# Attention beside an MLP on one core: one visit per head pair on 64x64 tiles, in place of separate phases

## The chip, the core and the metric

The kernel runs on one core of a Trainium2 chip. The metric is the device time of one execution in microseconds, the median of several runs. A profile is one further execution, and its span is a little shorter than the timed value. Engines are named as in the profile: PE (TensorE, the matrix engine), PEld (its weight loads), DVE (VectorE), ACT (ScalarE), POOL (GpSimd) and SP (SyncE, which here only issues transfers).

## What is computed

64 heads (8 batches of 8), each with 576 positions of 64 numbers. Every head has two attentions whose results are added: one over the means of four neighbouring positions (144 by 144), and one in which a position sees only neighbours less than four away. The result is the input of an MLP with a SiLU gate.

```python
q_d = q.reshape(B, H, Sd, factor, D).mean(axis=3)          # factor 4, likewise k_d, v_d
out_up = np.repeat(sm_attn(q_d, k_d, v_d), factor, axis=2)
mask = np.abs(pos[:, None] - pos[None, :]) < factor
scores = np.where(mask, scale * np.matmul(q, k.transpose(0, 1, 3, 2)), -1e9)
... softmax of scores ...
x = (out_up + np.matmul(attn, v)).transpose(0, 2, 1, 3).reshape(B * S, H * D)   # 4608 x 512
h = x @ w_in                                                # 512 x 2048
out = (h * (1.0 / (1.0 + np.exp(-h)))) @ w_out              # 2048 x 512
```

## The kernel before

Heads are worked on in pairs (32 pairs, 4 per batch). The program is written as one list of instructions per engine, with waits derived from what each reads and writes; a small scheduler in the source decides the order with rough costs. A pair goes through separate phases on PE, each with its own shape of tile. The phases of the pairs share two PSUM tiles, `duo0` and `duo1`, of two banks each; the MLP has `hps` (first layer, two banks) and `ops` (second layer, two banks).

```python
def load_v(p):                         # local attention: five overlapping windows of 128 keys
    win = bass.AP(..., ap=[[64, 128], [112 * 64, 5], [1, 64]])      # per head, into vs[128, 10, 64]
    ...                                # and vq[72, 4, 256]: four positions a row, for the means

def ph_T(p):                           # 6 + 6 transposes of 96 positions x 128 (both heads), then
    tps[:, 96 * c:96 * c + 96] <- transpose(w, id_bf)               # copies: q on DVE, k on ACT
def ph_S1(p):                          # scores, keys in rows: tiles 64x128, 2 heads side by side
    for c in range(4):
        for h in range(2):
            mm(D[:, h, QB[c]:QB[c] + NQ[c]], kT[rows, W0[c]:W0[c] + 128], qT[rows, ...])  # 120 or 112
def ph_S2(p): ...                      # fifth block, and 4 matmuls of 64x72 tiles for the means
# ACT: exp into Pt[128, 2, 576] and Pd[72, 2, 2, 144]; DVE: Pt *= mask
def ph_Z(z):                           # row sums of TWO pairs: 16 matmuls, tiles 128x32, weights all one
    mm(D[o:o + 32, 0, 0:360], ones_bf[:, 0:32], Pt[m][:, h, 0:360])
    mm(D[o:o + 32, 1, 0:216], ones_bf[:, 0:32], Pt[m][:, h, 360:576])
    for s in range(2):
        mm(D[o:o + 32, 1, 216:360], fours_bf[:, 0:32], Pd[m][:, h, s, :])
# ACT copies them to zc, 4 transfers bring them to zr[40, 72], DVE takes the reciprocal rr,
# 1 transfer writes it to DRAM (scr), 4 transfers read it back into Rb, spread over 64 partitions
def ph_PV(p):                          # 14 matmuls, tiles 128x64 (72x64 for the means)
    mm(D[64*h:64*h+64, ...], vb[:, 5 * h + c, :], Pt[:, h, QB[c]:QB[c] + NQ[c]])
    # DVE: xo = D * Rb in two instructions; POOL: xT = xo (local) + xo (means, four times each)
```

The first four pairs get their reciprocals another way: row sums into `hps`, a reciprocal on DVE, and a matmul that spreads them over partitions into `ops`.

```python
def g1(j, f):                          # first layer: 144 groups of four matmuls of 512 columns
    for kc in range(4): mm(hps[hb], w_in_sb[:, kc, 128*f:...], xT[:, kc, t0:t0 + 512])
    # ACT: th = tanh(h / 2); DVE: gT = (th + 1) * h
def g2(j, i):                          # second layer: 144 groups of four matmuls of 512 columns
    for f in range(4 * part, 4 * part + 4): mm(ops[ob], gT[:, f, 128*tt:...], w_out_bf[:, f, :])
    # after four groups ACT: osb = ops * 0.5, then a transfer to the output
```

The main loop of the scheduler takes an attention phase when one is ready (the same tile shape first), and an MLP group otherwise. Buffers: q and k 2 deep, v 2 deep, Pt and Pd 5, Rb 4.

The softmax here doesn't subtract the row's maximum and nothing guards it: scores larger than these inputs give would overflow.

## Time and profile before

| what | value |
|---|---|
| time, median of 3 runs | 417.98 us (415.85 to 418.28) |
| span of the profiled execution | 414.6 us, 6872 instructions |
| busy, share of span | PE 86%, PEld 52%, DVE 58%, ACT 52%, POOL 40% |
| largest groups on PE | hps 576 matmuls of 128x512, ops 576 (538 in the records) |
| chain that ended last, by engine | PE 58%, DMA 24%, SP's queue 5%, ACT 4%, DVE 3% |
| transfers | 65.62 MB in 80635 packets, of which 46812 under 512 B |
| sizes per transfer | vs 160 KB (x64), qs, ks and vq 288 KB (x32 each), Rb 180 KB (x56), output 256 KB (x36) |

How to read it: the busy share of PE is an average over a stage in which data is loaded, a stage in which attention and MLP share the engine, and a last stage of MLP alone. A matmul's record contains the time that it spends in the pipeline, so records overlap and PE looks busier than it is; counts of matmuls in a stretch of time say more. A share of a chain is the time of the steps that led, one releasing the next, to the last instruction.

### The profile page before, as it was taken

How to read it: one execution, taken by the hardware profiler on the slowest of the kernel's cores; microseconds unless marked ns; L12 is line 12 of the kernel's file. 1: busy time of each engine (PE TensorE's matmuls, PEld its weight loads, DVE VectorE, ACT ScalarE, POOL GpSimd, SP SyncE). 2: the span in 40 equal slices, each digit the busy share in tenths (PEclk: the TensorE clock that was granted, in tenths of full speed). 3: DMA queues.
4: the chain of work that ended last, by engine and by line, in shares of the span. 5: the costliest groups of instructions: out<-in, count | busy, mean ns of one | idle time of the engine just before them, and what ended most of it. 6: DMA issues, size and time to landing. Idle time of an engine off the chain costs nothing.

```text
span 414.6 us, 6872 instructions
## 1 busy us (share of the span) xinstructions
PE 356.2 (86%) x2682; PEld 215.0 (52%) x2720; DVE 240.9 (58%) x358; ACT 217.1 (52%) x375; POOL 165.4 (40%) x194
## 2 busy tenths in 40 slices
PE   3745467597939999999799999999999999999996
PEld 2422245364517656555455656565565555555552
DVE  4956334467646789687588776786546333333320
ACT  5551345356645767667578559648543344344331
POOL 7177185364436664567548277328004000000000
PEclk9968568988957999999999999999999999999999
DMA  7999999998568768989898994753151100101012
GB/s 209 258 217 321 224 216 213 209 202 217 160 185 201 183 161 187 251 178 225 208 235 204 231 248 106 211 159 78 53 145 52 52 25 25 52 25 51 27 51 76
DMA packets 80635, 65.62 MB, mean 158 GB/s; under 512 B 46812, under 2 KB 70364, under 8 KB 80604
## 3 DMA queue, kind: packets, MB, share of 16 engines
q1 hardware_dynamic: 75480, 57.38, 56.7%
q0 software_dynamic: 4224, 6.29, 6.7%
q10 hardware_dynamic: 900, 1.52, 1.4%
q8 instruction: 21, 0.34, 0.4%
q14 instruction: 10, 0.08, 0.1%
HBM read 57.51 MB, written 9.60 MB: 162 GB/s over the span
## 4 chain that ended last, share of the span: by engine, by line
PE 58%; DMA 24%; SPq 5%; ACT 4%; DVE 3%; issue 2%; POOL 2%; ACTq 1%; POOLq 0%
PE ops L340 26%; PE hps L340 24%; DMA vs<-in_v_dram 7%; DMA vq<-in_v_dram 6%; PE duo L340 5%; DMA scr<-rr 4%; DMA Rb<-scr 3%; PE duo L350 2%; DMA zr<-zc 2%; SPq L293 2%; ACT th L545 2%; DVE gT L547 2%; SPq L442 1%; DMA ks<-in_k_dram 1%; POOL vt L321 1%
## 5 line engine op out<-in xcount | busy, mean ns | idle before, releaser
L340 PE MATMUL hps<-xT,w_in_sb 128*128 128x512 f32 x576 | 180.2, 440 | 9.3 <-DVE gT L547 9.3
L547 DVE SCALAR_TENSOR_TENSOR gT<-th,hps 128x512 bf16<-128x512 f32 x144 | 98.3, 686 | 114.9 <-ACT th L545 114.5
L340 PE MATMUL ops<-w_out_bf,gT 128*128 128x512 bf16 x538 | 140.3, 383 | 6.2 <-DVE gT L547 2.6
L545 ACT ACTIVATE th<-hps 128x512 f32<-128x512 f32 x144 | 85.5, 597 | 105.4 <-PE hps L340 100.8
L340 PEld LDWEIGHTS hps<-xT,w_in_sb 128*128 128x128 f32 x576 | 109.0, 195 | 42.7 <-DVE gT L547 12.5
L340 PEld LDWEIGHTS ops<-w_out_bf,gT 128*128 128x128 bf16 x576 | 46.5, 98 | 66.9 <-issue 22.1
L522 POOL TENSOR_TENSOR xT<-xo 128x576 fp32r<-128x576 f32 (+2 forms) x40 | 40.2, 1018 | 79.5 <-DVE xo L505 79.2
L321 POOL TENSOR_TENSOR vt<-vq 72x512 f32<-72x512 f32 x32 | 43.0, 1342 | 32.3 <-DMA vq<-in_v_dram 31.2
L316 ACT ACTIVATE vb<-vs 128x640 bf16<-128x640 f32 x32 | 23.3, 735 | 29.6 <-DMA vs<-in_v_dram 26.4
L340 PE MATMUL duo<-qT,kT 64*128 64x112 bf16 (+1 forms) x320 | 21.5, 230 | 20.0 <-ACT Pd L391 7.3
L311 POOL CAST qb<-qs 96x768 bf16<-96x768 f32 x28 | 24.2, 865 | 33.0 <-PE duo L350 17.1
L397 DVE TENSOR_TENSOR Pt<-Pt,mask_bf 128x1152 bf16<-128x1152 bf16 x32 | 32.2, 1011 | 8.3 <-ACT Pt L389 8.3
L374 ACT ACTIVATE Pt<-duo 128x912 bf16<-128x912 f32 x32 | 29.5, 927 | 9.8 <-issue 4.9
L340 PEld LDWEIGHTS duo<-qT,kT 64*128 64x128 bf16 x320 | 11.5, 100 | 40.3 <-DVE xo L503 9.3
L566 ACT ACTIVATE osb<-ops 128x512 f32<-128x512 f32 x36 | 21.6, 599 | 19.5 <-PE ops L340 19.3
L355 DVE COPY qT<-duo 128x576 bf16<-128x576 bf16 x32 | 23.8, 748 | 13.4 <-PE duo L350 13.4
L350 PE MATMUL duo<-id_bf,qb 96*128 96x96 bf16 x192 | 15.5, 225 | 16.6 <-ACT Pt L374 8.0
L503 DVE TENSOR_TENSOR xo<-duo,Rb 128x456 f32<-128x456 f32 x32 | 20.0, 626 | 10.8 <-DMA Rb<-scr 6.2
L323 POOL TENSOR_TENSOR vd<-vt 72x256 bf16<-72x256 f32 x32 | 24.8, 776 | 2.5
L356 ACT ACTIVATE kT<-duo 128x576 bf16<-128x576 bf16 x32 | 20.8, 649 | 8.2 <-PE duo L350 8.2
L311 POOL CAST kb<-ks 96x768 bf16<-96x768 f32 x28 | 23.7, 845 | 2.7 <-DMA ks<-in_k_dram 2.7
L361 DVE TENSOR_REDUCE kd<-kT 128x144 bf16<-128x576 bf16 x32 | 23.8, 743 | 0.3 <-ACT kT L356 0.3
(48 smaller groups left out, 256.5 us busy)
## 6 DMA issues: line engine op xcount, KB each, us to landing
vs<-in_v_dram SPq DMA_DIRECT2D x64, 160.0 KB, 4.7
qs<-in_q_dram SPq DMA_DIRECT2D x32, 288.0 KB, 5.6
ks<-in_k_dram SPq DMA_DIRECT2D x32, 288.0 KB, 6.1
vq<-in_v_dram SPq DMA_DIRECT2D x32, 288.0 KB
out_dram<-osb SPq DMA_DIRECT2D x36, 256.0 KB, 2.2
Rb<-scr SPq DMA_DIRECT2D x48, 180.0 KB, 4.1
w_in_sb<-in_moe_w_in_dram POOLq DMA_DIRECT2D x4, 1024.0 KB, 13.1
w_out_bf<-in_moe_w_out_dram POOLq DMA_DIRECT2D x4, 512.0 KB, 10.7
```

Source lines behind the costliest of these rows:

```text
L311: pool(lambda g, d=dst, s=src: g.tensor_copy(d, s), r=[R(f"{nm}s{i}")], w=[R(f"{nm}b{j}")], cost=830)
L321: pool(lambda g: g.tensor_tensor(vt[:, :, :], vq[i][:, :, 0:128], vq[i][:, :, 128:256], ALU.add), r=[R(f"vq{i}")], w=[R("vt")], cost=1290)
L323: pool(lambda g: g.tensor_tensor(vd[m][:, :, :], vt[:, :, 0:64], vt[:, :, 64:128], ALU.add), r=[R("vt")], w=[R(f"vd{m}")], cost=750)
L340: return P.op("PE", lambda t: t.matmul(out_, lhsT, rhs, start=start, stop=stop, skip_group_check=True), r, w, cost=cost)
L350: P.op("PE", lambda t, c=c, w=w, tps=tps: t.transpose(tps[:, 96 * c:96 * c + 96], w, id_bf[:, :]), r=[R("id"), R(f"{nm}b{j}")], w=[bk[x]], ...
L355: P.op("DVE", lambda e: e.tensor_copy(dst[0], src[0]), r=[bk[0]], w=[R(f"qT{j}")], cost=800)
L361: P.op("DVE", lambda e: e.tensor_reduce(dst[j][:, :], src[j][:, :].rearrange("p (g r) -> p g r", r=4), mybir.AxisListType.X, ALU.add), r=[ ...
L374: P.op("ACT", lambda e: e.activation(Pt[m][:, :, 0:456], D[:, :, 0:456], AF.Exp, scale=0.125), r=bk, w=[R(f"P{m}")], cost=930)
L397: P.op("DVE", lambda e: e.tensor_tensor(Pt[m][:, :, :], Pt[m][:, :, :], mask_bf[:, :].unsqueeze(1).to_broadcast([128, 2, S_]), ALU.mult), ...
L522: P.op("POOL", lambda e, dst=dst, in0=in0, in1=in1: e.tensor_tensor(dst, in0, in1, ALU.add), r=[R(f"xo{x}")], w=xblk(kc, t, e_), cost=200 ...
L545: P.op("ACT", lambda e: e.activation(th[tb][:, :], hps[hb][:, :], AF.Tanh, scale=0.5), r=[R(f"h{hb}", True)], w=[R(f"th{tb}")], cost=600)
L547: P.op("DVE", lambda e: e.scalar_tensor_tensor(gT[j % 2][:, f, :], th[tb][:, :], 1.0, hps[hb][:, :], ALU.add, ALU.mult), r=[R(f"h{hb}", Tr ...
```

## The change

Attention is rewritten so that all its matmuls have one tile shape, 64x64: the array then holds four tiles, one for each half of the rows and each half of the columns, and four matmuls can run side by side. The local attention works on blocks of 48 queries and 64 keys, six blocks in each half of the sequence. The row sums are made with one-hot weights: a column of ones at a shifting place puts the sums of 36 queries into one row of PSUM, so that the 720 sums of a head lie in 10 rows of 72, and the reciprocal works on 72 numbers per partition; it goes to DRAM and back in one write and two reads, for every pair.

PE works on attention in one visit per step, a single burst without a change of tile shape, and the visit takes from each of four pairs one stage: values of pair n-2, row sums of pair n-1, scores of pair n, transposes of pair n+1. After a visit come four groups of the MLP's first layer and four of its second. The order on all engines is fixed by a new scheduler over units. PSUM is divided anew: AB for scores, CD for row sums and values, pe_ and o0 for transposes (o0 is also the second layer's bank), hps as before. Buffers: q and k together 4 deep, v windows 4, vq 2, Pt and Pd 4, Rb 3.

The diff replaces most of the file; its core, cuts marked by "...":

```diff
-        qs = sb("qs", [96, 2, 384], F32, NST)
-        ks = sb("ks", [96, 2, 384], F32, NST)
-        vs = sb("vs", [128, 10, 64], F32, NSTV)
-        vq = sb("vq", [72, 4, 256], F32, NSTV)
+        qk = sb("qk", [128, 2, 576], F32, NQK)
+        vs = sb("vs", [128, 12, 64], F32, NVS)
+        vq = sb("vq", [128, 4, 256], F32, NVQ)
...
+        def pe_T(u, p):
+            j = p % NB
+            for r in range(9):
+                for x, (t, rk) in enumerate(((o0, rF), (pe_, rE))):
+                    for h in range(2):
+                        o = t[half(h), 0:288].bitcast(BF16)[:, 64 * r:64 * r + 64]
+                        w = qkb[j][half(x), h, 64 * r:64 * r + 64]
...
+        def pe_S(u, p):
...
+            for i in range(6):
+                for h in range(2):
+                    for y in range(2):
+                        t = 288 * y + 48 * i
+                        mm(u, AB[half(y), h, 48 * i:48 * i + 48], kT[j][half(h), t:t + 64],
+                           qT[j][half(h), t:t + 48], rl, [rAB[h]])
+            for h in range(2):
+                for y in range(2):
+                    mm(u, AB[half(y), h, 288:432], kd[j][half(h), 64 * y:64 * y + 64], qd[j][half(h), :], rd, [rAB[h]])
+            for h in range(2):
+                for y in range(2):
+                    mm(u, AB[half(y), h, 432:504], kd[j][half(h), 128:192], qd[j][half(h), 72 * y:72 * y + 72],
+                       rd, [rAB[h]])
...
+                for s in range(8):                     # row sums of 36 queries into row s
+                    for h in range(2):
+                        for j in range(2):
+                            mm(u, CD[half(h), j, 360:396], 
+                               oh1[half(j), 63 - s:127 - s] if s else ohf[half(j), :],
+                               Pt[m][half(j), h, 36 * s:36 * s + 36],
...
+                for i in range(6):                     # values
+                    for h in range(2):
+                        for j in range(2):
+                            mm(u, CD[half(h), j, 48 * i:48 * i + 48], vb[n][half(j), 6 * h + i, :],
+                               Pt[m][half(j), h, 48 * i:48 * i + 48], [R(f"vb{n}"), R(f"P{m}")], [rCD[j]],
...
+            one("DVE", f"r{p}", 0.75, lambda e: e.reciprocal(zr[i][:, :, :], CD[:, :, 360:396]),
+                r=rCD, w=[R(f"zr{i}")], prio=-4)
+            eng = "ACT" if p < NACT else "SP"
+            dma(eng, f"z{p}", scr[u][:, :], zr[i][:, :, :].rearrange("p x n -> p (x n)"),
+                [R(f"scr{u}")], f"scr{u}", 0.18, r=[R(f"zr{i}")], prio=-5)
+            for h in range(2):
+                src = bass.AP(tensor=scr[u].tensor, offset=scr[u].offset + 64 * h * 72, ap=[[0, 64], [1, 720]])
+                dma(eng, f"b{p}", Rb[u][half(h), :], src, [R(f"Rb{u}{h}")], f"Rb{u}{h}", 0.72,
...
+        def V(n):
+            pv = n - 2 if n - 2 < NPAIR else None
+            z = n - 1 if n - 1 < NPAIR else None
...
+            pe_cross(u, pv, z)                         # means: the parts that cross the halves
+            if n < NPAIR:
+                pe_S(u, n)
+            if n + 1 < NPAIR:
+                pe_T(u, n + 1)
+            pe_main(u, pv, z)
...
+        for n, m in zip(range(6, 10), (3, 3, 2, 2)):
+            V(n)
+            feed()
+            G1(m)
+        for n in range(10, 46):
+            if n < NPAIR + 2:
+                V(n)
+                feed()
+            j, tt = divmod(n - 10, 4)
+            bank, rb = (o0, rF) if n < NPAIR or n % 2 else (pe_, rE)
+            G1(1)
+            g2(j, tt, 0, bank, rb)
+            G1(1)
+            g2(j, tt, 1, bank, rb)
+            G1(1)
+            g2(j, tt, 2, bank, rb)
+            g2(j, tt, 3, bank, rb)
+            G1(1)
```

Ahead of visit 6 the first pairs go through the same stages singly (T, S, Z and PV), with six groups of the first layer among the last of them. In the visit a pair has 36 transposes of 64 columns, 24 score matmuls of 48 columns with 4 of 144 and 4 of 72 for the means, 48 row-sum matmuls of 36 columns, and 24 value matmuls of 48 columns with 12 of 72 for the means.

## The prediction

> **What bounds the kernel now.** I read the slices of the span first, then tables of stages for the three PSUM tiles that TensorE writes, then the chain, and last the timeline of one small-matmul burst. The slices (rows PE, TensorE clock, DMA share, GB/s; each slice 10.4 us) show three stages:
>
> ```profile
> PE   3745467597939999999799999999999999999996
> ...
> PEclk9968568988957999999999999999999999999999
> DMA  7999999998568768989898994753151100101012
> GB/s 209 258 217 321 224 216 213 209 202 217 160 185 201 183 161 187 251 178 225 208 235 204 231 248 106 211 159 78 53 145 52 52 25 25 52 25 51 27 51 76
> ```
>
> To about 100 us the DMA queues are full (nines) while PE has gaps: loading bounds. From 150 to 250 us PE reads nine, but a matmul record contains its wait in the pipeline, so I count matmuls instead. Tables of 100, 50 and 50 us follow; in each the first column after the length is PE with its count, the second the weight loads. First hps (MLP first layer, plus 48 early row sums), then ops (second layer, plus 16 early broadcasts), then duo (all other attention):
>
> ```profile
> 0.00:100.00 100.00, 24.07 (x112) 15.10 (x112) 20.34 (x20) 9.21 (x16) 0.81 1.05 229
> ...
> 150.00:200.00 50.00, 23.54 (x78) 14.25 (x79) 13.21 (x20) 11.35 (x19) 1.00 0.83 197
> 200.00:250.00 50.00, 22.87 (x76) 13.42 (x75) 12.68 (x19) 11.31 (x19) 1.00 0.91 219
> ```
>
> ```profile
> 0.00:100.00 100.00, 17.61 (x38) 7.01 (x40) 4.72 (x17) 0.81 1.05 229
> ...
> 150.00:200.00 50.00, 18.04 (x68) 5.98 (x76) 2.99 (x5) 1.00 0.83 197
> 200.00:250.00 50.00, 17.98 (x69) 5.94 (x76) 2.40 (x4) 1.00 0.91 219
> ```
>
> ```profile
> 0.00:100.00 100.00, 23.18 (x340) 16.41 (x340) 13.06 (x22) 22.10 (x36) 0.81 1.05 229
> ...
> 150.00:200.00 50.00, 12.79 (x284) 8.81 (x280) 9.29 (x16) 16.44 (x27) 1.00 0.83 197
> 200.00:250.00 50.00, 13.02 (x280) 9.17 (x280) 11.47 (x21) 14.89 (x25) 1.00 0.91 219
> ```
>
> The chain gives the price of undisturbed MLP work, groups of four matmuls:
>
> ```profile
> 352.24 0.88 PE ops L340 x4
> 353.12 0.93 PE hps L340 x4
> ```
>
> So between 150 and 250 us PE did 154/4 = 38.5 first-layer groups and, by weight loads, 152/4 = 38 second-layer groups: 38.5 x 0.93 + 38 x 0.88 = 69.2 us. The other 30.8 us went to attention, its changes of tile shape and its waits. One pair has 48 duo matmuls (12 transposes, 14 scores, 14 values, half of 16 row sums), so 564/48 = 11.75 pairs: **2.6 us of PE per pair, one pair every 8.5 us**, beside only 3.3 + 3.2 MLP groups. By 100 us there were done (112-48)/4 = 16 first-layer groups, (40-16)/4 = 6 second-layer groups and 340/48 = 7.1 pairs. Check: what then remained, 128 x 0.93 + 138 x 0.88 + 24.9 x 2.6, is 305 us; 100 + 305 + 3.2 of tail (the last matmul of the chain ends at 411.4) is 409 of 414.6, the rest being waits from 100 to 150 us. After loading, the end is set by MLP work plus what attention costs on PE.
>
> **What the Trainium skill says.** "TensorEngine Tiling (Array Packing)", Key Properties: tiles of a divided array run independently, and a change of tiling mode drains the array. The trace agrees: in the row-sum burst below, four 128x32 tiles start within 0.02 us, and PE is given back only 0.6 us after the start although the columns take 0.37. "TensorE: Matmul & The Clock Gate", in its passage on 56 ns against 53.3: starts never come closer than about 25 ns however few the columns. Nothing here tests that for matmuls under 72 columns, which are most of the new ones. "DMA: Bandwidth & Descriptors", Anatomy of one DMA: about 2 us of every transfer is fixed. The trace agrees for the output (2.2 us to landing); the broadcast Rb takes 4.1.
>
> **The change, part by part.**
>
> *Small matmuls.* Timeline rows of one burst, start, length, operation:
>
> ```profile
> 195.20 0.43 PE L340 MATMUL duo<-Pt,ones_bf 128*32 128x360 bf16 x8 [0.50 <-DVE Pt L397]
> 195.46 0.30 PE L340 MATMUL duo<-Pd,fours_bf 72*32 72x144 bf16 x8
> 195.79 0.50 PE L340 MATMUL hps<-xT,w_in_sb 128*128 128x512 f32 x1
> ```
>
> Sixteen matmuls on four tiles stream 360 + 216 + 2 x 144 = 864 columns per tile; at 512/0.22 = 2330 columns per us that is 0.37 us, and the next work starts 0.59 us after the first: 0.22 us for entering and leaving. The new visit has 160 matmuls in quartets: transposes 9 x 64, scores 6 x 48 + 144 + 72, row sums 12 x 36, values and their cross terms 6 x 48 + 3 x 72 columns, together 2016, or 0.87 us. Forty quartets at an estimated 5 to 10 ns of start add 0.2 to 0.4, one entry and exit 0.22 (against some seven shape changes per pair before): **1.3 to 1.5 us; I take 1.5**, against 2.6. It holds no wait of its own, because a visit works on four different pairs.
>
> *Order.* Sixteen first-layer groups precede the visit that the source numbers 10; from there each visit is followed by 4 + 4 groups, 4 x (0.93 + 0.88) = 7.24 us, so 8.74 us per pair while 24 visits last, then MLP alone.
>
> *Loading.* Per pair: q and k 0.59 MB as before; v windows 12 instead of 10 (0.39 for 0.33 MB); downsampled v 0.33 for 0.29; Rb 0.37 for every pair. The early pairs no longer get their reciprocals through PE, so they need Rb too. Visit 10 needs q and k of 12 pairs (7.1 MB) and Rb of 9 (3.3); with v prefetched to about 10.5 pairs (7.6) and the weights, 6.3 MB in the software queue's row, that is 24.3 MB. At the first ten slices' mean, 229 GB/s, this is 106 us; with landing, **visit 10 at 108 us**.
>
> *VectorE, ScalarE, GpSimd per period of 8.74 us*, from the rows before: VectorE 4 x 0.686 (gate) + 2 x 0.74 (means) + half of 1.01 (mask) + 0.6 (reciprocal) + 1.0 (scaling) = 6.3; ScalarE 4 x 0.60 + 0.60 + 2 x 0.65 + 0.88 (v cast, 12/10 of 0.735) + about 1.15 (exponentials of 1008 columns in place of 1.94 for 1728) = 6.3; GpSimd 1.3 + 1.34 + 0.78 + 1.2 = 4.6. None becomes the bound; VectorE has 2.4 us to spare.
>
> *Row-sum round trip.* Reciprocal 0.6 plus its queue about 0.6, issue 0.35, write 2.5 to 6.0 (pieces of scr in the chain), issue of two Rb halves 1.2, landing 4.1: about 10 to 12 us. The scaling is needed a visit later, 8.7 us, but stands behind two gate instructions and a mask, about 3 us more. It nearly fits; I charge 0.25 us per visit, 6 in all.
>
> *Sum.* 108 + 128 x 0.93 (119.0) + 144 x 0.88 (126.7) + 22 full and two half-empty visits (34) + waits 6 + tail 3.2 = 397 us of span. The timed median lies 3.4 above the profiled span (417.98 - 414.6): **400 us**. Against before: 8 us later out of loading and 5 us more second layer left, against 31 us saved in visits.
>
> **Rivals.**
> - *The visit is bound by starts or instruction supply, not columns.* For: 320 PE instructions per visit, with their weight loads of 64 columns; the instruction queue moves 16 KB a packet (0.34 MB in 21), and a visit is 20 KB at 64 bytes each (an estimate: 0.34 MB over the 5402 PE instructions). Against: quartets start together in the burst. At 2.6 us a visit the time is 424, at 3.5 about 444.
> - *DMA stays the bound after 108 us.* A period moves 1.68 MB plus 0.26 of output in 8.74 us, 222 GB/s; before sustained 197 to 219 from 150 to 250 us without being full (0.83, 0.91). At 210 a period is 9.2 us: 411.
> - *The round trip comes late.* SP issues 13 transfers per pair at 0.35 to 0.6, about 6 us, and stands still while scr is written; a pair that waits 1 us on VectorE gives 418.
> - *Loading costs less than I think*, because four-deep buffers keep the queues full from the start and 2304-byte packets replace 1536-byte ones: visit 10 at 98, 390 us.
>
> **Range and chances.** The middle is 400. The good side needs earlier loading and 1.4 us visits: 378. The bad side is one rival at moderate size: 428. The border of 2% is 409.6, only one rival away; a visit under 1.9 us keeps the other steps within it. Faster 0.64, same 0.18, slower 0.18.
>
> **What would show it.** Right: visit bursts of 1.3 to 1.6 us from first transpose or score to the next MLP matmul; visit 10 between 100 and 112 us; 8.7 to 9.2 us from visit to visit; VectorE waits for Rb under 10 us in all; MLP groups still 0.93 and 0.88. Wrong: bursts of 2.5 us or more at full clock; PE waiting for gT while VectorE waits for Rb; DMA share at one until 300 us; or a first MLP group well after 60 us.

## The result, and the profile after

The changed kernel takes **429.6 us** (median of four runs, 428.9 to 431.7) against 417.5 of the kernel before, timed beside it: 1.028 times the time, 95% interval 1.023 to 1.033. It is slower, and 1.6 us above the predicted range (378 to 428).

The slices of the changed kernel, in the same rows as before (PE, TensorE clock, DMA share; each slice 10.7 us):

```profile
PE   1332326467389989987998899999999999999997
...
PEclk9999999778769989996999899999999999999999
DMA  8999999996978899879989899865222211010111
```

PE stays below five tenths for the first six slices and first reads nine in slice 13, at 128 us. In slices 10 and 12 (96 to 107 and 118 to 128 us) the DMA engines are *not* full, so by then it is no longer plain loading. The clock falls in slice 8 and is low in places until slice 19.

The table for hps (MLP first layer), in the three windows of the prediction; first the length, then PE with its count, then the weight loads, VectorE, ScalarE, the clock, the DMA share, GB/s:

```profile
0.00:100.00 100.00, 16.34 (x48) 10.93 (x48) 6.58 (x10) 6.29 (x12) 0.95 1.10 230
150.00:200.00 50.00, 20.93 (x70) 14.25 (x70) 12.05 (x18) 10.20 (x18) 0.90 0.92 215
200.00:250.00 50.00, 22.79 (x78) 15.26 (x78) 12.78 (x19) 11.55 (x20) 0.96 0.94 219
```

By 100 us there are 12 first-layer groups and no second-layer group; before there were 16 and 6. From 150 to 250 us there are 148/4 = 37, against 38.5 before.

The prediction's own stages begin where the score bursts start in PE's timeline: visit 10 at 119.6 us, visit 23 at 257.0, visit 31 at 328.5. Whole-core rows for them (length; PE, PEld, DVE, ACT, POOL busy; clock, DMA share, GB/s):

```profile
0.00:119.60 119.60, 48.58 (x1588) 37.23 (x1591) 53.99 (x80) 40.65 (x65) 55.43 (x81) 0.91 1.06 224
119.60:257.00 137.40, 127.27 (x2511) 84.57 (x2505) 75.06 (x118) 76.35 (x130) 61.83 (x66) 0.93 0.91 215
257.00:328.50 71.50, 71.06 (x1541) 46.67 (x1544) 45.41 (x72) 45.65 (x78) 30.64 (x33) 1.00 0.54 143
```

The middle stage holds 13 periods of 10.57 us: 127.27/13 = 9.79 busy and 0.78 idle. The last stage holds eight of 8.94, nearly all busy, at full clock. Predicted were 8.74 for every period. The first MLP group came at 69.3 us (55.7 before): the prediction had named "well after 60 us" as a sign of being wrong.

Undisturbed MLP work costs what it did. The chain of the changed kernel, near the end of its visits (start, length, what):

```profile
341.15 0.88 PE pe_ L331 x4
342.03 0.93 PE hps L331 x4
```

One visit, from PE's timeline, shortened to its first and last rows (start, length, instruction):

```profile
205.60 0.23 PE L331 MATMUL CD<-Pd,vd 64*64 64x72 bf16 x4
...
207.26 0.26 PE L331 MATMUL CD<-Pd,vd 64*64 64x72 bf16 x8
207.45 0.50 PE L331 MATMUL hps<-xT,w_in_sb 128*128 128x512 f32 x1
```

From the visit's first matmul to the next MLP matmul it is 1.85 us; 1.5 was predicted.

The waits up to visit 10, then those in the middle stage (who waited for whom: us in total, times, longest):

```profile
DVE xo L624 <- DMA Rb<-scr: 22.5, 6, 5.5
...
PE CD L331 <- DVE xo L624: 19.5, 4, 7.3
```

```profile
DVE xo L624 <- DMA Rb<-scr: 20.9, 10, 5.5
...
PE CD L331 <- DVE xo L624: 13.1, 7, 4.4
```

VectorE waits for the returned tile Rb (43.4 us over the whole span), and while it waits, the scaling has not freed the one pair of accumulators CD, so PE waits too. The prediction had named the sign: waits for Rb under 10 us in all would have spoken for it. Of the 13.1 us, 3.1 lie just before 119.6; the other 10.0 are practically all of PE's idle time in the middle stage (137.40 - 127.27 = 10.1).

The longer of these gaps are paid twice. Two of them in PE's timeline (the gap in brackets), then the windows right after (columns as in the whole-core rows, the clock third from the end):

```profile
195.48 0.28 PE L331 MATMUL CD<-Pd,vd 64*64 64x72 bf16 x4 [4.44 <-DVE xo L624]
...
237.17 0.23 PE L331 MATMUL CD<-Pd,vd 64*64 64x72 bf16 x4 [2.54 <-DVE xo L624]
```

```profile
193.90:200.70 6.80, 5.22 (x167) 4.57 (x168) 4.08 (x7) 1.79 (x3) 3.90 (x4) 0.50 1.12 227
...
238.30:241.70 3.40, 3.40 (x66) 2.84 (x60) 1.88 (x4) 1.60 (x3) 2.55 (x4) 0.50 1.06 217
```

In the records of this kernel the clock is either 1.00 or 0.50. From 81 to 242 us there are six half-clock stretches, from 81.3, 101.7, 112.0, 152.9, 193.9 and 238.3 us on, each 3 to 14 us long, and each begins during a gap of 1.8 to 5.4 us in PE's work or within 1.5 us after one. Not every such gap is followed by one (in e13 below, one of 2.8 us at 141.6 is not).

The outputs show when the time is lost. Start of the issue of an output transfer, from the timelines:

| output transfer | before, us | after, us | difference |
|---|---|---|---|
| 8th | 188.0 | 207.3 | 19.3 |
| 16th | 269.0 | 287.7 | 18.7 |
| 28th | 366.5 | 382.1 | 15.6 |
| 36th, the last | 412.1 | 425.5 | 13.4 |

All of the loss is there by the eighth of 36 outputs; after it the changed kernel wins back 6 us.

### The profile page after: what moved, and what is told of

It is laid out like the page before. It is cut to its first block, busy times and chain, and to the rows that moved or that the text cites. A ratio compares the mean times of both kernels' runs of the same rounds, so it can differ in the third digit from the quotient of the medians.

```text
span 428.0 us, 14106 instructions
## 1 busy us (share of the span) xinstructions
PE 343.0 (80%) x6272; PEld 225.2 (53%) x6272; DVE 209.1 (49%) x319; ACT 199.5 (47%) x335; POOL 151.7 (35%) x182
## 4 chain that ended last, share of the span: by engine, by line
PE 55%; DMA 24%; SPq 9%; DVE 4%; issue 3%; ACT 2%; ACTq 2%; POOL 1%; POOLq 0%; DVEq 0%
PE hps L331 23%; PE o L331 16%; DMA scr<-zr 11%; SPq L401 9%; DMA Rb<-scr 8%; PE CD L331 6%; PE pe_ L331 6%; DMA vq<-in_v_dram 3%; PE AB L331 2%; ACTq L401 1%; DMA qk<-in_k_dram 1%; DVE xo L624 1%; PE o L492 1%; POOL vt L478 1%; DVE zr L609 1%
## 5 line engine op out<-in xcount | busy, mean ns | idle before, releaser
L331 PE MATMUL hps<-xT,w_in_sb 128*128 128x512 f32 x576 | 168.9, 435 | 11.6 <-DVE gT L669 11.6
L331 PEld LDWEIGHTS hps<-xT,w_in_sb 128*128 128x128 f32 x576 | 112.5, 200 | 42.0 <-DVE gT L669 7.7
L331 PE MATMUL o<-w_out_bf,gT 128*128 128x512 bf16 x464 | 108.2, 380 | 0.6 <-issue 0.4
L651 POOL TENSOR_TENSOR xT<-xo 128x576 fp32r<-128x576 f32 (+3 forms) x48 | 42.9, 908 | 119.1 <-DVE xo L624 119.0
L331 PEld LDWEIGHTS o<-w_out_bf,gT 128*128 128x128 bf16 x464 | 41.8, 98 | 58.0 <-issue 9.1
L624 DVE TENSOR_TENSOR xo<-CD,Rb 128x720 f32<-128x720 f32 x32 | 28.7, 896 | 52.7 <-DMA Rb<-scr 43.4
L478 POOL TENSOR_TENSOR vt<-vq 128x512 f32<-128x512 f32 x32 | 41.2, 1287 | 28.7 <-DMA vq<-in_v_dram 28.0
L467 POOL CAST qkb<-qk 128x1152 bf16<-128x1152 f32 x30 | 34.3, 1144 | 15.6 <-issue 6.8
L502 ACT ACTIVATE kT<-pe_ 128x576 bf16<-128x576 bf16 x32 | 20.7, 646 | 33.1 <-issue 14.3
L480 POOL TENSOR_TENSOR vd<-vt 128x256 bf16<-128x256 f32 x32 | 23.7, 740 | 32.7 <-PE CD L331 31.6
L609 DVE RECIPROCAL zr<-CD 128x72 f32<-128x72 f32 x32 | 19.4, 607 | 26.7 <-PE CD L331 26.7
L331 PE MATMUL CD<-Pd,vd 64*64 64x72 bf16 x384 | 16.6, 217 | 14.1 <-DVE xo L624 13.1
L472 ACT ACTIVATE vb<-vs 128x768 bf16<-128x768 f32 x32 | 27.2, 850 | 0.1
L492 PE MATMUL o<-idn,qkb 64*64 64x64 bf16 x576 | 18.8, 211 | 10.6 <-DVE qkb L462 5.7
L331 PE MATMUL pe_<-w_out_bf,gT 128*128 128x512 bf16 x112 | 26.4, 380 | 0.0
L533 ACT ACTIVATE Pt<-AB 128x576 bf16<-128x576 f32 x32 | 20.7, 647 | 11.5 <-PE CD L331 8.6
L334 ACT ACTIVATE qT<-o 128x576 bf16<-128x576 bf16 x24 | 15.6, 650 | 20.9 <-PE pe_ L492 19.9
```

The source lines that it names most:

```text
L331: L.op(u, lambda t: t.matmul(out_, lhsT, rhs, start=start, stop=stop, skip_group_check=True), r, w)
L467: one("POOL", f"c{p}", 1.2, lambda g: g.tensor_copy(qkb[j][:, :, :], qk[i][:, :, :]), r=[R(f"qk{i}0"), R(f"qk{i}1")], w=[R(f"qkb{j}0"), R( ...
L472: one("ACT", f"cw{p}", 0.86, lambda e: e.activation(vb[m][:, :, :], vs[i][:, :, :], AF.Copy), r=[R(f"vs{i}{h}{j}") for h in range(2) for j ...
L478: one("POOL", f"va{p}", 1.3, lambda g: g.tensor_tensor(vt[:, :, :], vq[i][:, :, 0:128], vq[i][:, :, 128:256], ALU.add), r=rr, w=[R("vt")])
L480: one("POOL", f"vb{p}", 0.76, lambda g: g.tensor_tensor(vd[m][:, :, :], vt[:, :, 0:64], vt[:, :, 64:128], ALU.add), r=[R("vt")], w=[R(f"vd ...
L609: one("DVE", f"r{p}", 0.75, lambda e: e.reciprocal(zr[i][:, :, :], CD[:, :, 360:396]), r=rCD, w=[R(f"zr{i}")], prio=-4)
```

## The experiments

Three theories were set against each other. **A**: SyncE's 13 issues per pair set the pace; in the middle stage its queue has hardly a gap. From its timeline (start, length, transfer, count; L401 is the one line that issues them):

```profile
119.95 0.63 SPq L401 DMA_DIRECT2D vs<-in_v_dram  x1
120.62 0.63 SPq L401 DMA_DIRECT2D qk<-in_q_dram  x1
121.30 1.31 SPq L401 DMA_DIRECT2D qk<-in_k_dram  x1
122.65 1.57 SPq L401 DMA_DIRECT2D vq<-in_v_dram  x3
...
```

The typical issue is 0.6 us, not the 0.35 to 0.6 of the prediction, and 13 of them are about 8 us. **B**: the return trip of the 1/sums (reciprocal, write to scr, read back into Rb) is late, and the visits wait. **C**: the bytes set the pace.

What the runs gave is collected here, by label. "Time" is the median; the ratio is against the kernel before, timed beside it. "Visit 10" and "23" are starts of score bursts; "period" is the mean between them. Busy and idle are PE's, per period, and clock is TensorE's mean, all in that stage. Executions more than 1.5% longer than the fastest of the same kernel are left out of times and ratios (so e1 has 423.1 here, where the recorded texts further down say 426); this leaves one of e14_early_pe (450.4 us), whose stages are not read, and the only profile of e21_pool_b is of such an execution (417.0 us), so its stages are not in the table.

| run | time | ratio (95%) | visit 10 | visit 23 | period | busy + idle | clock |
|---|---|---|---|---|---|---|---|
| changed kernel | 429.6 | 1.028 (1.023 to 1.033) | 119.6 | 257.0 | 10.57 | 9.79 + 0.78 | 0.93 |
| e1_nowait | 423.1 | 1.013 (1.004 to 1.022) | 111.1 | 241.3 | 10.02 | 9.48 + 0.54 | 0.97 |
| e5_v_act | 458.6 | 1.098 (1.090 to 1.106) | 155.9 | 287.1 | 10.09 | 9.25 + 0.84 | 0.98 |
| e6_half_v | 423.0 | 1.010 (1.007 to 1.013) | 116.0 | 250.3 | 10.33 | 9.39 + 0.94 | 0.97 |
| e4_later | 436.0 | 1.043 (1.034 to 1.052) | 120.8 | 250.6 | 9.99 | 9.06 + 0.93 | 0.93 |
| e9_v_act_mid | 434.4 | 1.041 (1.035 to 1.048) | 124.3 | 260.7 | 10.49 | 9.45 + 1.04 | 0.95 |
| e10_no_trip | 410.6 | 0.982 (0.974 to 0.990) | 95.3 | 226.6 | 10.10 | 9.23 + 0.87 | 0.98 |
| e11_loads_once | 386.6 | 0.926 (0.922 to 0.931) | 93.0 | 209.8 | 8.98 | 8.89 + 0.09 | 1.00 |
| e2_chain_act | 437.7 | 1.050 (1.043 to 1.057) | 116.5 | 254.8 | 10.63 | 9.39 + 1.24 | 0.96 |
| e12_small_trip | 416.6 | 0.999 (0.995 to 1.002) | 106.9 | 235.0 | 9.86 | 9.42 + 0.44 | 0.97 |
| e13_bf16_trip | 421.6 | 1.011 (1.008 to 1.015) | 111.7 | 248.4 | 10.51 | 9.55 + 0.96 | 0.96 |
| e15_early_bf16 | 443.4 | 1.063 (1.048 to 1.078) | 109.3 | 258.9 | 11.51 | 10.04 + 1.47 | – |
| e16_plan | 423.0 | 1.013 (1.001 to 1.024) | 112.5 | 248.8 | 10.48 | 9.50 + 0.98 | 0.95 |
| e17_plan_bf16 | 417.9 | 1.005 (1.002 to 1.008) | 106.7 | 243.0 | 10.48 | 9.37 + 1.11 | 0.96 |
| e18_plan_bf16_vact | 416.2 | 1.004 (1.001 to 1.008) | 110.5 | 243.9 | 10.26 | 9.52 + 0.74 | 0.96 |
| e19_no_stop | 424.3 | 1.023 (1.014 to 1.032) | 106.7 | 238.7 | 10.15 | 9.51 + 0.64 | 0.96 |
| e20_early_plan | 456.8 | 1.100 (1.092 to 1.107) | 112.8 | 266.8 | 11.85 | 10.32 + 1.53 | – |
| e21_pool_b | 413.3 | 0.995 (0.992 to 0.998) | – | – | – | – | – |

Two things limit what a row can show. First, the source lays out the order of every engine's list by a simulated timeline, so an edit that takes away a wait or a transfer, or moves it to another engine, also changes the orders. Of VectorE's 319 instructions only 220 come in the same sequence in e1 as in the changed kernel, and 228 in e16, which changes nothing but the order. The same lists stand on VectorE, ScalarE, GpSimd and SyncE only in four pairs of rows: changed kernel and e13, e16 and e17, e1 and e12, and, but for 12 small memsets, changed kernel and e6. These pairs differ in bytes. Second, visits and periods are read from one execution per kernel, while the times of one kernel spread over up to 6 us.

### First four: one wait, some issues, some bytes, one visit later

**e1_nowait** scales with a constant and leaves the softmax division out; all transfers stay.

```diff
-  Rb[u][:, :].rearrange("p (m x n) -> p x m n", x=2, n=36), ALU.mult),
-  r=rCD + [R(f"Rb{u}0"), R(f"Rb{u}1")], w=[R(f"xo{x}")])
+  Rc[:, :].rearrange("p (m x n) -> p x m n", x=2, n=36), ALU.mult),   # Rc: ones
+  r=rCD + [R("Rc")], w=[R(f"xo{x}")])
```

> The scaling reads a constant tile of ones in place of the 1/sums that come back from DRAM. All transfers, the reciprocal included, are kept; the softmax division is left out of the result. In the changed kernel VectorE waits 43.4 us for the returned tile and TensorE 29.5 us for the scaling to free the accumulators. Theory B (the return trip is what the visits wait for): the waits of TensorE for the scaling fall under 5 us, visit 10 comes before 112 us instead of 119, the pairs from visit 10 to 23 come every 9.0 to 9.3 us instead of 10.6, and the whole takes 400 to 410 us. Theory A (SyncE's 13 issues per pair set the pace): the pairs still come every 10.1 to 10.6 us, with new waits for q and k or v in place of those for the returned tile, and the whole takes 422 to 428. Theory C (the bytes set the pace): as A, with the DMA engines still busy above 0.90.

Visit 10 came 8.5 us sooner (111.1), as B said; some of that can be the changed order, which alone moved visit 10 by 7.1 us in e16. The middle fell by 0.55 us a period only. Even with no wait for Rb, PE is busy 9.48 us of each. So the run supports B for the start; in the middle it gained half a microsecond of the 1.8 that are missing. From visit 23 on this run was slower (10.05 us a period against 8.94) and gave back more than half of its lead of 15.7 us. So did the other runs without the division, e10, e12 and e19 (10.45, 9.78 and 10.58), and e11 took 9.49 there; why stays open.

**e5_v_act** takes four of SyncE's 13 issues away.

```diff
-  dma("SP",  f"lv{p}", d[:, lo:hi, :], win, ...)
+  dma("ACT", f"lv{p}", d[:, lo:hi, :], win, ...)
```

> The four loads of v windows of each pair are issued by ScalarE instead of SyncE, so SyncE issues 9 transfers per pair instead of 13; bytes, shapes and everything else as in the changed kernel. Theory A (SyncE's issues set the pace, about 0.62 us each, near 8.2 us per pair plus its own waits): SyncE shows gaps, the pairs from visit 10 to 23 come every 9.0 to 9.5 us instead of 10.6, the whole takes 405 to 418 us. Theory B (the return trip through DRAM is late for its own reasons): the median time of the two small transfers stays at 3.5 and 4.5 us each and the period falls by 0.5 us at most, 422 to 430. Theory C (bytes): the period stays within 0.2 us of 10.6, with the DMA engines busy above 0.90, 426 to 431.

The start was spoilt: ScalarE's own list now held loads ahead of its first casts, and the first score burst came at 28 us instead of 11. The middle stage can still be read. SyncE issued there for 55% of the time instead of 94%. The stage row, then the waits in it:

```profile
155.90:287.10 131.20, 120.31 (x2504) 78.76 (x2504) 73.97 (x116) 76.02 (x130) 58.49 (x62) 0.98 0.90 201
```

```profile
PE o L331 <- issue: 7.8, 5, 2.0
...
DVE xo L624 <- DMA Rb<-scr: 2.8, 2, 1.4
```

The waits for Rb all but vanish (20.9 to 2.8 us), and still the period is 10.09. PE's idle time is no smaller (0.84 us a period against 0.78); 7.8 us of it stand before second-layer groups ("o"), and the profile names no releaser for them. Theory A falls as the bound of this stage: with nearly half of SyncE free, the gain is half a microsecond. The page "DMA: Bandwidth & Descriptors" of the Trainium skill says in its section Issuing engines are not separate DMA queues that issuing from several engines saves no more than the sequencer's time to initiate. This trace agrees: with two issuing engines the DMA engines are 0.90 busy in this stage, with SyncE alone 0.91.

**e6_half_v** loads three of six windows per v transfer (`hi = 3` in `load_v` for pairs 1 to 30), so half of the v windows of those pairs are left out.

> For pairs 1 to 34 the loads of v windows fetch three of six windows each, so the same number of transfers with 0.197 MB less per pair (of about 2.2 MB in each period of the middle stage); the other three windows hold zeros or an older pair's values, so that part of the attention is left out. Theory C (bytes): 0.197 MB at 215 GB/s is 0.9 us, so the pairs of visit 10 to 23 come every 9.6 to 9.8 us instead of 10.6, and the whole takes 408 to 416 us. Theory A (number of issues): unchanged to 0.3 us, 423 to 430, unless the time of an issue falls with the elements in it. Theory B: the small transfers land a little sooner, the period falls by 0.2 to 0.5 us, 418 to 427.

(The text above says pairs 1 to 34; there are 32, and the first and the last load in full.) Visit 10 came 3.6 us sooner, the period fell by 0.24 us, not by 0.9, although the DMA engines were busy 0.77 instead of 0.91. With the same lists on both sides, theory C falls as the bound of the middle stage.

**e4_later** gives the trip a period more: products with v three visits after the scores.

```diff
-  pv = n - 2 if n - 2 < NPAIR else None
+  pv = n - 3 if 4 <= n - 3 < NPAIR else None          # and one more buffer for Pt, Pd, vb, vd, Rb
```

> The products with v of a pair come one visit later (three visits after its scores instead of two), with one more buffer each for the weights, v and the returned tile, so that the 1/sums have a whole period more to come back; the computation is complete. Theory B: the waits of VectorE for the returned tile fall from 43 us to under 15, those of TensorE for the scaling from 29.5 to under 10, the period from visit 10 on falls to 9.2 or less, the whole takes 405 to 416 us although one visit comes later at the end. Theory A: the waits move to q, k and v; the period stays at 10.1 or more, the whole 424 to 432. Theory C: as A.

The waits for Rb fell to 26.7 us, and visit 23 came 6 us sooner. But the start did not move, and the last score burst was followed by 107.7 us instead of 99.5, because one visit and its MLP groups come later. Its shorter period (9.99) is no gain either: in those 13 periods it did 48 first-layer groups, the changed kernel 53. Slower in sum.

### What is left without loads, and without the trip

**e9_v_act_mid** is e5 from pair 12 on (`"ACT" if p >= 12 else "SP"`).

> The loads of v windows are issued by ScalarE from pair 12 on only, so that the start is left as it is and SyncE has 9 issues per pair in the middle stage; the computation is complete. The earlier run that moved them from the first pair on lost 30 us at the start, but its middle stage had SyncE busy 54% of the time and waits of VectorE for the returned tile of 2.8 us. If SyncE's issues delay the return trip (theory A and B together): visit 10 stays at 117 to 121, the pairs from visit 10 to 23 come every 9.6 to 10.1 us instead of 10.6, the waits for the returned tile in that stage fall from 21 to under 6 us, the whole takes 415 to 424. If the clock and TensorE's own work set the middle stage: 10.1 to 10.5 and 423 to 430, with the idle time of TensorE there under 6 us of 137. If bytes: 10.4 to 10.7.

The period was 10.49, and the start was later than expected (124.3). Relieving SyncE is no help here either.

**e10_no_trip** deletes the three transfers of the trip and scales with ones: the division is left out.

> Neither the transfer of the 1/sums to DRAM nor the two that bring them back: VectorE scales with a tile of ones (the division is left out), SyncE has 10 issues per pair in place of 13, and 0.41 MB per pair of traffic is gone (of about 2.0). The run with the tile of ones but all transfers came to visit 10 at 111, 10.0 us per pair to visit 23, 426 in all. Theory A: SyncE needs 10 x 0.6 = 6 us per pair, so the middle falls to 9.1 to 9.4 (TensorE's own work) and the whole to 395 to 405. Theory C: 0.41 MB at 218 GB/s is 1.9 us, so no more than TensorE's own work is left either: the same, and visit 10 comes 8 to 12 us sooner, at 100 to 104. If TensorE's own work with a reduced clock sets it: the middle stays at 9.7 to 10.0 and the whole at 410 to 418.

Visit 10 at 95.3, 24 us sooner: far more than the 7.1 us of order alone in e16, so the trip in some form makes most of the slow start. The middle stayed at 10.10, against all three theories; the branch "TensorE's own work with a reduced clock" (9.7 to 10.0, 410 to 418) came closest.

**e11_loads_once** returns at once from `load_qk`, `load_v` and `load_vq` for pairs from 4 on; attention then works on old data.

> q, k and v are loaded for pairs 0 to 3 only, later pairs work on what lies in the buffers (their attention is of old data); the return trip, the weights and the output are kept. SyncE has 4 issues per pair, and 1.27 MB per pair less is moved. What is left is TensorE's work, the return trip and the chain from casts to visits. Theory: the period from visit 10 on is TensorE's own 4 x 0.93 + 4 x 0.87 + 1.7 to 1.85 = 8.9 to 9.1 us at full clock; visit 10 comes at 75 to 85, and the whole takes 370 to 385. If the return trip itself is long without any load in the queues: waits for the returned tile stay above 15 us and the period above 9.5. If the lower clock comes with the work itself: the period is 9.5 or more with TensorE hardly idle.

This is the floor. Its stage rows:

```profile
93.00:209.80 116.80, 115.58 (x2503) 77.41 (x2514) 78.53 (x119) 77.04 (x132) 57.41 (x62) 1.00 0.24 77
209.80:285.70 75.90, 70.68 (x1536) 46.45 (x1543) 45.49 (x72) 45.66 (x78) 30.71 (x33) 1.00 0.22 71
```

13 periods in 116.8 us, 8.98 each, with 0.09 idle, at a clock of 1.00. Visit 10 came at 93.0, not at 75 to 85, so the loads of the later pairs are not all of the start. Its visit in PE's timeline, first and next MLP matmul:

```profile
173.76 0.23 PE L331 MATMUL CD<-Pd,vd 64*64 64x72 bf16 x4
...
175.29 1.20 PE L331 MATMUL hps<-xT,w_in_sb 128*128 128x512 f32 x4
```

That is 1.53 us. So PE's own work is what the prediction said, 8.98 against 8.74, and what lies beyond it does not appear without the loads (their bytes, their issues and the waits that they lengthen all go at once here). The return trip, which this run keeps, is no wait of its own in that stage either: without loads in the queues the write of scr landed in 1.5 us and Rb in 3.7 (medians in its middle stage), against 3.5 and 4.5 in the middle stage of the changed kernel and 7.0 and 6.9 in its start.

**e2_chain_act** issues the trip from ScalarE for every pair (`eng = "ACT"`).

> The return trip's three transfers are issued by ScalarE for every pair, not only for the first 8: SyncE has 10 issues per pair, and the trip doesn't queue behind loads; the computation is complete. Theory A and B together: the waits for the returned tile in the middle stage fall from 21 us to under 6, the period from 10.6 to 9.7 to 10.1, the whole 415 to 424. Against it: ScalarE stands still while the first transfer lands (3.5 us) unless other work is ahead of it, and each stop delays the Tanh and the exponentials: if that wins, waits of TensorE for gT and of VectorE for Tanh grow and the period stays at 10.5 or more, 428 to 445.

Its last branch came true: period 10.63, slower in sum. Idle time of PE in the middle grew to 1.24 us a period.

### The trip's bytes, and the early pairs

**e12_small_trip** is e1 with `[1, 72]` in place of `[1, 720]` in the two broadcast reads (the division is left out).

> As the run with the tile of ones (the division is left out), but each of the two transfers that bring the 1/sums back fetches 72 of 720 columns: the same 13 issues per pair, 0.33 MB per pair less. The run with all transfers came to visit 10 at 111 us and took 426; the one without the trip's transfers came there at 95 and took 410.5. If bytes set the start (theory C): visit 10 comes at 95 to 100 and the whole takes 408 to 414. If the number of issues and the landing of small transfers do (theory A): visit 10 stays at 107 to 112, the whole at 422 to 427.

Visit 10 at 106.9, just under the range of theory A, and the time between the two. Against e1, with the same lists, the bytes account for 4.2 of the 15.8 us that lie between e1 and e10 at visit 10, for 6.3 of 14.7 at visit 23, and for 6.5 us of the time.

**e13_bf16_trip** computes everything, with coarser 1/sums: `zr`, `scr` and `Rb` in BF16.

> The reciprocals, their copy in DRAM and the returned tile are bf16 instead of f32: half the bytes of the trip (0.2 MB per pair less), the same issues; the computation is complete, with a coarser 1/sum. If bytes set the start: visit 10 comes 6 to 9 us sooner, at 110 to 114, the middle stage a little faster, the whole 417 to 423. If issues: 427 to 431.

Visit 10 came 7.9 us sooner, about what the bytes of nine pairs, 1.83 MB, take at 229 GB/s (8.0); the middle did not change (10.51). All of the gain was made in the start, as C said of that stage. That the sizes agree may be luck: by the same sum e12 should have gained 13 us (3.0 MB), and gained 4.2.

**e14_early_pe** and **e15_early_bf16** give pairs 0 to 3 their 1/sums by PE, as the kernel before did.

```diff
+  if p < 4:                          # sel: rows of ones, one 64x64 block per row of sums
+      for m in range(10): for h in range(2):
+          mm(v, hps[b][half(h), 72*c:72*c + 72], sel[half(h), 64*m:64*m + 64], zb[i][half(h), ...])
+      # ScalarE copies hps to Rb; no trip
```

> Pairs 0 to 3 get their 1/sums as in the kernel before, without the trip: TensorE spreads the reciprocals over the partitions with 20 matmuls against rows of ones, into the banks that the MLP doesn't use yet, and ScalarE copies them to the tile that the scaling reads. Later pairs are as in the changed kernel; the computation is complete, with the early 1/sums in bf16. In the changed kernel the first scaling comes at 39 us, the next ones about 9 us apart, and the first MLP group at 69. If the trip behind a full queue is what delays the start (theory B there): the first MLP group comes at 55 to 60, visit 10 at 107 to 112, the whole takes 418 to 423. If loads alone set it: the first MLP group at 64 to 69, visit 10 at 112 or later, the whole 424 to 430.

> Both of the last two: pairs 0 to 3 without the trip, the later ones with a trip in bf16. The computation is complete. If bytes and the trip's wait each take their share of the start: visit 10 at 100 to 106, the whole 409 to 417, faster than either kernel. If only one of them counts: 418 to 423.

In e15 visit 10 came at 109.3, only 2.4 us before e13's. After that the visits came unevenly, often 15 us and then 9 or 10 us apart, with a mean of 11.5. The order differs here too, so these two say little of the early pairs themselves.

### The order, and the stop of the issuing engine

The scheduler in the source orders each engine's list by a simulated timeline, in which a transfer costs 0.42 us to issue and lands 1.6 us after its turn. **e16_plan** changes these figures and nothing else:

```diff
-  def dma(eng, name, out_, in_, w, sem, dcost, r=(), prio=None, cost=0.42):
+  def dma(eng, name, out_, in_, w, sem, dcost, r=(), prio=None, cost=0.6):   # and 1.18 * dcost
-  u.end = ring[e] + 1.6
+  u.end = ring[e] + 3.5
```

**e17_plan_bf16** adds the trip in bf16, **e18_plan_bf16_vact** also v from ScalarE from pair 12.

> The kernel lays out each engine's instruction order from a simulated timeline. Three of its figures are set to what the runs show: 0.6 us for an issue instead of 0.42, landing 3.5 us after a transfer's turn instead of 1.6, and transfers 18% longer (215 GB/s). Instructions, bytes, issues and the computation are those of the changed kernel; only orders differ. If orders that don't fit the real landings cause the waits: the waits for the returned tile fall from 43 us to under 25, visit 10 comes at 105 to 114, the pairs to visit 23 every 9.6 to 10.2 us, the whole 410 to 422. If bytes and the clock set it whatever the order: 426 to 432, with visit 10 near 119 and 10.4 us or more per pair.

> The order laid out as in the last one, and the trip in bf16 (which alone brought visit 10 to 112 us and the whole to 422). The computation is complete. If order and bytes add: visit 10 at 100 to 107, the whole 403 to 415, faster than both kernels. If the order is of no use: 419 to 424.

> As the last one, with the loads of v windows issued by ScalarE from pair 12 on: SyncE has 9 issues per pair. The computation is complete. With an order laid out for it, theory A says that the middle stage gains another 0.3 to 0.6 us per pair against the last one, 398 to 411; if the issues don't matter, or ScalarE's work is delayed by them as in the run with v on ScalarE from pair 12 (434), it is within 1% of the last one or slower.

The order alone moved visit 10 by 7.1 us, to 112.5, and the time to 423.0; the middle period (10.48) stayed, and the waits for Rb fell to 36.7 us only, not under 25. With bf16 visit 10 came at 106.7 and the whole was within half a per cent of the kernel before; four issues fewer on SyncE (e18) changed the time by less than 1%. So two kernels with the same instructions and bytes differ by about 1.5% through order alone (the intervals of their ratios just touch), and the gain is again in the start. The same change of figures in the kernel with the bf16 trip (e13 to e17) gained 3.7 us.

What makes the early trip so dear shows in ScalarE's timeline of the changed kernel, which issues the trip for pairs 0 to 7 (in brackets the idle time before, and what ended it):

```profile
30.50 0.56 ACTq L401 DMA_DIRECT2D scr<-zr  x1
...
33.62 0.53 ACT L535 ACTIVATE Pd<-AB 128x432 bf16<-128x432 f32 x1
40.04 1.29 ACTq L401 DMA_DIRECT2D Rb<-scr  x2
42.17 0.33 ACTq L401 DMA_DIRECT2D scr<-zr  x1
42.54 0.65 ACT L502 ACTIVATE kT<-pe_ 128x576 bf16<-128x576 bf16 x1 [8.40 <-PE CD L331]
50.14 1.10 ACTq L401 DMA_DIRECT2D Rb<-scr  x2
51.28 0.65 ACT L533 ACTIVATE Pt<-AB 128x576 bf16<-128x576 f32 x1 [8.09 <-PE CD L331]
```

From the issue of the write to that of the read 8 to 9.5 us pass, and the engine stands for 6 to 7 of them (34.1 to 40.0, 43.2 to 50.1): the read may not be issued before the write has landed, and the list is in order. Copies of kT and exponentials of later pairs stand behind it. "DMA: Bandwidth & Descriptors", Two DMAs through the same engine are not ordered, says that the issuing engine has to wait for the first transfer's semaphore; here is what that wait costs the other work of that engine. **e19_no_stop** takes the stop away from e1 and keeps all transfers (the division is left out; the order of the lists changes with it):

```diff
-  src = bass.AP(tensor=scr[u].tensor, offset=scr[u].offset + 64 * h * 72, ap=[[0, 64], [1, 720]])
+  src = bass.AP(tensor=q.tensor, offset=q.offset + 64 * h * 72, ap=[[0, 64], [1, 720]])   # waits for zr only
```

> As the run with the tile of ones (the division is left out), and the two broadcast transfers read 720 columns of q instead of the copy in DRAM, so they wait for nothing that has to land first. Number, shape, bytes and engine of all transfers are the same. With the tile of ones alone: first MLP group at 60.5, visit 10 at 111, 426 in all; without the trip's transfers 58, 95 and 410.5. If the stop of the issuing engine is what costs: visit 10 at 97 to 104, the whole 410 to 418. If bytes and issues cost: visit 10 at 108 to 112, the whole 421 to 427.

Visit 10 came at 106.7, 4.4 us before e1's, which misses the branch "stop" (97 to 104) and the branch "bytes" (108 to 112) alike. The stop is real, as the timeline above shows, but what it costs the whole isn't shown: 4.4 us is less than order alone moved. In its timeline the reads follow the write at once:

```profile
26.64 0.33 ACTq L403 DMA_DIRECT2D scr<-zr  x1
27.00 1.16 ACTq L403 DMA_DIRECT2D Rb<-in_q_dram  x2
```

The whole was no faster than e1 (424.3 against 423.1): the periods after visit 23 took 10.6 us each, and before some first-layer groups there PE stood for about 2 us that the profile puts down to no releaser.

**e20_early_plan** joins early pairs by PE with e18; **e21_pool_b** is e17 with the two reads of every trip issued by GpSimd, and so the stop too.

> Pairs 0 to 3 get their 1/sums through TensorE, the trip of the others is in bf16, v is issued by ScalarE from pair 12, and the order is laid out with the measured figures (all but the first was in the run that took 416.4). The computation is complete. ScalarE then stops for pairs 4 to 7 only. If the stop costs about 2 us a pair: visit 10 at 99 to 105 instead of 110.5, the whole 404 to 412, faster than both kernels. If the order goes wrong after the start, as in the earlier two runs with early pairs through TensorE (16 us from visit to visit every second time): 425 or more.

> The two transfers that bring the 1/sums back are issued by GpSimd for every pair, the write of them by ScalarE for the first 8 pairs and by SyncE later; bf16 trip and the order laid out with measured figures as in the run that took 418. The computation is complete. GpSimd is busy 35% and now bears the stop. If the stop on ScalarE was the cost of the start: visit 10 at 98 to 106, the whole 405 to 414. If GpSimd's casts and sums are delayed by as much: visit 10 at 107 or later, the whole 416 to 430.

e20 fell into the same uneven visits as e15. e21 took **413.3 us**, 0.995 times the kernel before (0.992 to 0.998): with the changed kernel's parts, a bf16 trip, an order laid out for real landings and the reads on GpSimd, the new attention comes out half a per cent ahead of the kernel before. It is 4.6 us under e17 in the medians, 1% by the ratios. That the gain lies in the start, as expected, is not shown: in its profile visit 10 came at 111.7, later than in e17, and visit 23 at 242.7, as there, while the waits for Rb fell to 6.8 us from 36.5.

## Why the prediction was wrong, step by step

- **The visit: right.** 1.5 us was taken; 1.53 without loads, 1.85 in the visit shown from the changed kernel's middle stage, at a clock of 1.00 (the others at full clock there took 1.62 to 1.85; what slows them is not shown). In its columns one term was short: a pair has 56 row-sum matmuls, not 48 (1792 in the records, for 32 pairs), so 14 x 36 columns instead of 12 x 36, and 2088 in all, 0.90 us instead of 0.87. The count of 160 was right. The rival "bound by starts or instruction supply" (2.6 us or more) did not come.
- **MLP groups 0.93 and 0.88: right** at full clock.
- **Loading, visit 10 at 108: near what was left without the trip's waits, but not what set it.** With the waits and the stop of the trip taken away and all bytes kept (e19), visit 10 came at 106.7; that it came so close is partly luck, since e19 also has another order. In the changed kernel it came at 119.6.
- **Row-sum round trip, "I charge 0.25 us per visit, 6 in all": this step failed.** Ahead of visit 10 the prediction charged the trip nothing but its bytes; there VectorE waited 22.5 us for Rb, and PE 19.5 us behind it. From visit 10 to 23 PE waited 10.0 us, about 0.75 a visit. Two terms were mis-sized for the start. Write and read were taken as 2.5 to 6.0 and 4.1 us; behind the full queues they landed in 7.0 and 6.9 (medians). And the engine that issues the read was not seen as standing still with other work behind it on ScalarE, 6 to 7 us each time. Leaving out the whole trip brought visit 10 to 95.3 (e10), halving its bytes to 111.7 with the same lists (e13). How much of the rest is wait (8.5 by e1) and how much stop (4.4 by e19) is not separated from the order. The rival "the round trip comes late" named the mechanism and gave it 418.
- **The sum has no term for the clock: the same failure, paid a second time.** The MLP and visits were priced at full clock. The middle stage ran at 0.93, because 19.6 of its 137.4 us ran at half clock, each time right after a gap in PE's work, and from 150 us on the gaps were waits for the scaling. PE was busy for 18.0 us of this time; half of that, about 9 us, is lost (an estimate that takes PE's pace as proportional to the clock). So of the 24 us that the middle stage took beyond 13 x 8.74, 10 are gaps and about 9 the clock after them; the rest is of the size of the slower visits. e11 has hardly a gap there, and a clock of 1.00. Loads alone do not lower the clock: the kernel before had 1.00 from 150 to 250 us with its DMA engines 0.83 to 0.91 busy.
- **"SP issues 13 transfers per pair at 0.35 to 0.6, about 6 us": too small, and it mattered little.** They take about 8 (median 0.61 each). The q loads of pairs 12 to 27 were issued 8.7 us apart, and 7.1 apart in e10 with 10 issues per pair. But that is faster than the visits came, so the lead of the q loads over their scores grew from 38 to 59 us, and SyncE at 55% did not bring the period under 10.
- **"DMA stays the bound after 108 us": not so.** Fewer bytes left the middle period nearly unchanged (10.33 in e6, 10.51 in e13, against 10.57).

After visit 23 the prediction had 397 - 221.6 = 175 us left; it took 428.0 - 257.0 = 171. So the whole miss arose before visit 23: 11.6 us before visit 10, 24 between.

**What stays open.** First, the middle stage. With loads in the queues no run came under 9.86 us per period, a figure that also needed the division left out. When one wait was removed, PE's idle time moved to another (0.4 to 1.5 us a period), and it vanished only without loads. That lists fixed in advance meet varying landing times is argued, not shown: the run with measured figures in the layout changed the start alone. Second, the parts of the trip at the start do not add up: wait 8.5, stop 4.4, bytes 4.2 by e12 (7.9 by e13), while leaving out all of it gains 24. They need not: e12, without the bytes, and e19, without the stop, both come to visit 10 at 107, and only e10, with neither, at 95, as two limits of about the same length would give. A run with the small trip and no stop, in one and the same order, would tell.

## What to carry to other kernels

A trip through DRAM inside a pipeline is to be priced with the landing times of the stage in which the queues are full, and its second issue charged to whatever stands behind it in the issuing engine's list. Where several resources are close to the bound (here PE, SyncE, the DMA engines), taking one away shows only half a microsecond, so look for a run that removes a whole class of work, as the one without loads did, before believing any single bound. And a list order laid out with a cost model is part of the kernel: measured figures in it were worth about 1.5% with no instruction changed. It also spoils experiments: an edit that removes one wait re-orders everything, so compare the lists before a difference is put down to the edit, or fix the order first. A mean clock under 1 is worth taking apart too: here it was gaps, paid again in the microseconds after them.

## What was not expected of the hardware

- Issue time on SyncE went with what stood just ahead of it, not with the load. Directly behind another issue the write of scr and an output took 0.59 us (medians, middle stage of the changed kernel). After a gap they took 0.33 and 0.34 in e11, and in e5, with the DMA engines 0.90 busy, the write of scr, always after a gap, took 0.34 (median of 13). On ScalarE it took 0.35 in the start, with the queues full.
- Landing times of the same small transfer spread by a factor of four or more: the 36 KB write of scr took 1.5 us with empty queues, 3.5 in the middle stage and 7.0 in the start (medians).
- A visit of 160 matmuls of 36 to 144 columns on 64x64 tiles took 1.53 us at full clock, under 10 ns a matmul on average. On each of the four tiles that is 38 ns from one to the next, so the least distance of about 25 ns that the prediction names was kept on each tile, and does not hold across tiles.
- The granted clock was 1.00 or 0.50 and nothing between; a mean of 0.93 over a stage was four short stretches at half.
